# Sparse attention and a mixture of experts on one core: value tiles of the last batch by DMA, and another order of the same work

## The chip, the cores and the metric

The kernel runs on one core of a Trainium2 chip. The metric is device time in microseconds (us), as the median of several runs. TensorE (PE, with its weight loads as PEld), VectorE (DVE), ScalarE (ACT), GpSimd (POOL) and SyncE (SP, which here only issues loads and stores) each work through a queue of their own in order, and wait for one another by semaphores.

## The reference

Attention over 4 batches, 8 heads, 768 positions, head size 64. A query sees the keys less than 16 positions away and one summary key for each block of 32 (24 of them); then an expert layer works on the 128 best positions of each batch.

```
k_sum = k.reshape(B, H, nb, 32, D).max(axis=3)
v_sum = v.reshape(B, H, nb, 32, D).mean(axis=3)
scores = concat([where(|i - j| < 16, scale * q @ k.T, -1e9), scale * q @ k_sum.T + log(32)])
a = softmax(scores)
x = a @ concat([v, v_sum])            # heads side by side: x is 4 x 768 x 512
top = 128 largest of x[b] @ w_gate    # per batch
out[b] = x[b]
out[b, top] += sigmoid(x[b, top] @ w_gate) * (relu(x[b, top] @ w1) @ w2)
```

## The kernel before, in words

Two heads make a pair; there are 16 pairs, four to a batch, numbered n = 0 to 15. A pair is worked in three steps of 256 queries, so there are 48 steps, i = 0 to 47. Steps 0 to 35 go pair by pair (batches 0 to 2). In the last batch the steps go round: 36 to 39 are the first step of pairs 12 to 15, 40 to 43 the second, 44 to 47 the third.

The work of every engine is written as small named operations, and one string, `ORDER`, lists their names in the order in which they are issued. A letter behind a colon picks the engine where there is a choice (v VectorE, s ScalarE, g GpSimd). Each engine takes its own operations out of this one list, in this order, and an operation that waits holds up all that stand behind it on its engine. Nothing else plans the work.

The names, with the lines of the profile:

- `q`, `k`, `vt`: loads of a pair's queries, keys and turned values (L194, L190, L201), on SP's queue. Four buffers each for q and k, two for vt.
- `kmax` (L213, VectorE), `spr` (L216 or L175): block maxima of the keys, copied ahead of every slice of the key tile. `vsum` (L224 on VectorE, or five halvings on GpSimd, L230), `ms` (L254, L256): block sums of the values, and their means, written ahead of every slice of the value tile.
- `vx` (L265, TensorE): turns four value windows (positions to partitions) for one step of a pair, into the PSUM bank "m"; `vk` (L268) copies that to the value tile v. There are four value tiles.
- `S` (L289, TensorE): the scores of two steps, 32 products. `M` (L301, VectorE): adds the mask and takes the row minimum of the negated scores. `E` (L312 on ScalarE, four instructions; L315 on VectorE or GpSimd, one instruction): the exponent, or on VectorE and GpSimd the subtraction alone, with the exponent taken by the next copy. `sm` has two buffers, p three.
- `T` (L321, TensorE): turns p, four transposes; `V` (L326, L328): copies it out, to pt. `A` (L338, TensorE): p times the values, 16 products. `R` (L343), `N` (L354, L357): reciprocal and scaling into x.
- `ga`, `gq`, `gl` (L393, L383, L388, VectorE): gate sums of x. `rt`, `rk`, `rw`, `rr`: the row of a batch's sums, turned by TensorE (L400), written to memory and read back to all partitions (L406, L409). `cmp` (L427, L429, VectorE): comparisons, `rank` (L438), `oh`, `pick`, `pk`: the chosen positions. `gat` (L474, GpSimd): gathers their rows from memory.
- The expert layer: `fgp` (L537, GpSimd), `fx`, `f1` (L561), `ft`, `f2` (L614), `fo`, and `sca` (L628, GpSimd), which scatters the result. `w`, `wh`, `wl` load the weights and split them into a high and a low part (L495 or L175, L499).
- `zero`, `warm` (L663): products of zeros at the start, which write the bank "m". `clrv`, `onep`, `ones`: tiles set to constants.

Another way for the values is in the code and unused before: `VMODE[n] == "d"`. There a pair loads plain turned values (`vt`, for `vsum` alone, L199) and two halves of the finished value tile from memory (`v`, L206); the means are turned by one small transpose (`mt`, L237), scaled (`mk`, L240) and copied by DMA from SBUF into the two halves (`md`, L248). `vx`, `vk` and `ms` are not used for such a pair. A tile of 24 rows, two buffers, lies between `mk` and `md`.

Of the kernel before, what the change touches and what calls it, by code (L numbers as in the profile page):

```python
# [55 lines left out]
vx0.0 clrv0:g vk0.0:s E0:g M1.0:v onep0:g vx0.2 vk0.2:s T0 k1 kmax1:v spr1:g V0:s q1 S2 M2.0:v E1:g M3.0:v M3.1:v E3:g  # L56
M2.1:v vt1 vsum1:v vx0.1 vk0.1:s T1 k2 kmax2:v A0 R0:v V1:s A1 R1:v S4 M5.1:v E2:g ms1:s vx1.0 M4.0:v M4.1:v E4:g q2
N0:s vt2 T2 V2:s T3 spr2:s vk1.0:v vx1.1 vk1.1:s M5.0:v E5:v V3:s S6 k3 kmax3:v M6.1:v vx1.2 T4 M7.1:v N1:s M7.0:v
M6.0:v V4:s A2 R2:v vsum2:g A3 R3:v vk1.2:s q4 T5 q3 ms2:s vx2.0 V5:s vk2.0:s spr3:g S8 E7:v M9.0:v E6:g M8.0:v M8.1:v
N2:v T6 vx2.1 N3:s A5 R5:v clrv3:g vk2.1:s M9.1:v w1 E8:v vx2.2 N5:v V6:s T7 A4 vt3 wh3:g E9:g vsum3:v ms3:g R4:v V7:s  # L60
N4:v wl3:g k4 kmax4:v S10 M10.1:v vk2.2:s T8 V8:s vx3.2 M11.0:v M10.0:v A7 vk3.2:s A6 M11.1:v T9 V9:s vx3.0 spr4:g S12
R7:v N7:v k5 vk3.0:s A9 kmax5:v R6:v E11:v M13.1:v E10:g M12.1:v N6:s R9:v vx3.1 vt4 vsum4:g ms4:g vk3.1:s N9:v
casts:v T10 M12.0:v V10:s A8 vx4.2 vk4.2:s T11 k6 q5 V11:s spr5:g M13.0:v E13:s kmax6:v gate R8:v N8:v S14 spr6:s
E12:g A10 ga0.0:v ga0.1:v w0 M14.1:v q6 M15.1:v vt5 vx4.1 vk4.1:s T12 V12:s wh1:g wl1:g A11 vx4.0 vk4.0:s T13 V13:s
M15.0:v E15:s q7 M14.0:v S16 R10:v N10:v A12 E14:g R11:v N11:v k7 ga0.2:v ga0.3:v ga0.4:v A13 ga0.5:v rt0 rk0:s
M17.1:v M17.0:v T14 M16.1:v vsum5:g ms5:g vx5.0 V14:s vt6 T15 R12:v vk5.0:s M16.0:v vx5.1 vk5.1:s S18 kmax7:v E16:v
N12:v A14 R13:v spr7:s st0.0 N13:v E17:g V15:s T16 vsum6:g w2 wh5:g M19.1:v M18.1:v ms6:g V16:s vx5.2 wh2:s M18.0:v
M19.0:v E19:v vk5.2:s rw0 A15 R14:v E18:v wh4:s wl4:g S20 M20.0:v vx6.2 wl2:g vk6.2:s M20.1:v M21.0:v M21.1:v R15:v
T17 N15:v V17:s k8 vx6.0 vk6.0:s st0.1 N14:s kmax8:v rr0 cmp0.5:v vt7 T18 V18:s E20:g S22 M22.0:v A16 R16:v q8 k9
E21:s N16:s vx6.1 vk6.1:s vt8 M22.1:v T19 vsum7:v spr8:g M23.1:v ms7:s V19:s A17 R17:v cmp0.1:v A18 q10 R18:v N18:v  # L70
wh0:g wl0:g M23.0:v vx7.1 N17:s vk7.1:s cmp0.3:v kmax9:v T20 V20:s E22:g cmp0.4:v cmp0.2:v A19 R19:v N19:v vx7.0 E23:s
T21 cmp0.0:v vsum8:g rb0:v S24 M25.1:v M24.1:v V21:s T22 vk7.0:s vx7.2 V22:s M25.0:v vk7.2:s A20 R20:v M24.0:v T23
V23:s q9 rank0 rs0:v oh0:v A21 spr9:s S26 R21:v N21:v st0.2 pick0 pk0:v w3 wl5:g vt9 N20:v E24:s T24 M26.1:v E25:g
M27.1:v ms8:g V24:s M27.0:v vx8.0 vk8.0:s M26.0:v A22 R22:v N22:v k10 A23 T25 V25:s vx8.1 vk8.1:s gat0:g fgp0:g
ga1.0:v S28 vx8.2 vsum9:v vk8.2:s R23:v N23:v wh7:s A25 ga1.1:v fx0 fxh0:s kmax10:v E26:g T26 V26:s A24 R25:v wh6:g
M28.0:v ms9:s wl6:g f10.0 M28.1:v E28:s f10.3 spr10:s fxl0:v E27:g M29.1:v M29.0:v ga1.2:v w4 wh8:s ga1.3:v st1.0
vx9.0 vk9.0:s T27 V27:s ga1.4:v ga1.5:v w5 wh10:g E29:s wl7:v S30 rt1 rk1:s M30.0:v M31.0:v T28 V28:s f10.4 M31.1:v
E31:v wl10:g k11 vx9.1 N25:s vt10 k12 vsum10:v R24:v f10.1 f10.2 q11 wh11:g vk9.1:s rw1 N24:v kmax11:v spr11:s T29
vx9.2 M30.1:v E30:v vk9.2:s A26 st1.1 V29:s wl11:g A27 kmax12:v spr12:s fge0:s R27:v N27:v R26:v N26:v S32 M32.1:v T30
V30:s M32.0:v wh9:g ms10:g M33.1:v vx10.0 vk10.0:s w7 wh14:s A28 E32:v rr1 f10.5 vx10.1 R28:v fr0.0:s ft0.0 wl9:g  # L80
wl8:g w6 wh12:s wh15:g wl15:g M33.0:v cmp1.4:v T31 A29 N28:v A30 cmp1.1:v k13 S34 vt11 V31:s T32 R29:v N29:s vk10.1:s
A31 cmp1.0:v fr0.1:s ft0.1 V32:s cmp1.5:v cmp1.3:v st1.2 cmp1.2:v rb1:v R30:v wl14:g rank1 wh13:g wl13:g wl12:g
fh0.0:s fl0.0:v fh0.1:s rs1:v E33:g T33 vx10.2 vk10.2:s V33:s f20.0 oh1:v pick1 k15 M35.1:v fl0.1:v pk1:v gat1:g k14
vsum11:v f20.1 M35.0:v kmax13:v E35:g f20.2 ms11:s spr13:g vx11.0 vk11.0:s N30:v f20.3 R31:v N31:s kmax15:v vx11.2
vk11.2:s f20.4 fg0:v fx1 kmax14:v spr14:s M34.1:v spr15:s M34.0:v A32 fxh1:v fxl1:v q12 fgp1:g E34:g fge1:s A33 R33:v
N33:s ga2.0:v q13 S36 M37.1:v M37.0:v ga2.1:v R32:v M36.0:v T34 V34:s f20.5 f11.0 M36.1:v vx11.1 T35 fo0.0:v E37:s q14
vk11.1:s N32:v f11.1 q15 S38 E36:s A34 fg1:v M38.1:v M39.1:v R34:v V35:s A35 N34:v vt12 vsum12:g ms12:s ga2.2:v R35:v
N35:v sca0:g T36 V36:s vx12.0 vk12.0:s vt13 f11.3 vx12.1 M39.0:v f11.2 vk12.1:s fr1.0:s vx12.2 vk12.2:s f11.4 T37
ga2.3:v ga2.4:v ga2.5:v vsum13:v rt2 M38.0:v rk2:s V37:s S40 ms13:g vx13.0 vk13.0:s ft1.0 fh1.0:s E39:v E38:g M40.1:v
M40.0:v T38 vx13.2 vk13.2:s M41.1:v fl1.0:v f11.5 M41.0:v E41:v fr1.1:v V38:s vt14 vsum14:g ms14:g vx13.1 E40:v rw2  # L90
S42 M42.0:v rr2 vk13.1:s A36 R36:v N36:v A37 R37:v M43.0:v T39 V39:s vt15 M43.1:v cmp2.4:v vx14.0 vk14.0:s ft1.1
fh1.1:s T40 E43:g vx14.1 vk14.1:s M42.1:v E42:g vsum15:v ms15:g V40:s A38 R38:v st2.0 S44 N37:s T41 V41:s cmp2.3:v
vx15.0 vk15.0:s N38:v f21.0 M45.0:v M44.1:v cmp2.0:v M44.0:v M45.1:v T42 E45:g vx15.1 cmp2.1:v A39 R39:v cmp2.2:v
N39:s vk15.1:v A40 cmp2.5:v S46 A41 V42:s T43 rank2 f21.1 R41:v E44:g M46.0:v rb2:v rs2:v N41:s R40:v N40:v st2.2
V43:s T44 V44:s vx15.2 M47.1:v vk15.2:s oh2:v M46.1:v A42 A43 M47.0:v R42:v N42:s pick2 pk2:v R43:v N43:v T45 vx14.2
vk14.2:v fl1.1:v E46:g A44 R44:v st2.1 V45:s A45 E47:s T46 f21.2 f21.3 V46:s R45:v N45:s T47 V47:s gat2:g fgp2:g
gq3.0:v gl3.0:v gq3.1:v gl3.1:v ro3.0 ri3.0:s gq3.2:v gq3.3:v f21.4 gl3.2:v N44:s gl3.3:v cmp3.0:v f21.5 fo1.0:v
cmp3.1:v sca1:g fge2:s fx2 fxh2:s A47 R47:v N47:s fxl2:v A46 R46:v f12.0 f12.1 N46:v ro3.1 ri3.1:s f12.3 gq3.4:v
gq3.5:v gl3.4:v gl3.5:v ro3.2 ri3.2:s cmp3.2:v cmp3.3:v cmp3.5:v cmp3.4:v f12.2 fr2.0:s st3.1 f12.4 ft2.0 f12.5 rank3
fh2.0:s fl2.0:v fr2.1:s ft2.1 rb3:v rs3:v oh3:v pick3 pk3:v fh2.1:s fl2.1:v f22.0 st3.2 f22.1 f22.2 fg2:v f22.3 f22.4  # L100
st3.0 gat3:g fx3 fxh3:v f22.5 fo2.0:v f13.0 sca2:g f13.3 fxl3:v f13.1 f13.2 fr3.0:s f13.4 f13.5 fr3.1:s ft3.0 fh3.0:v
ft3.1 fl3.0:v fh3.1:v f23.3 f23.0 f23.1 fgp3:g fge3:s fl3.1:v f23.2 f23.4 fg3:v f23.6 f23.7 f23.5 f23.8 fo3.0:v f23.9
f23.10 f23.11 fo3.1:v sca3:g
"""


# [1 line left out]
def attn_moe(ctx: ExitStack, tc: tile.TileContext, q, k, v, vt, vs, w1, w2, cst, line, out, cap):  # L108
# [109 lines left out]
    def value_sums(e, n):  # L218
        vv = vtb[n % 2][:, 0:S].rearrange("p (u c) -> p u c", u=NU) if VMODE[n] == "d" else own(by_slot(vtb[n % 2]))
        vv = vv.rearrange("p u (m t) -> p u m t", t=BLK)  # L220
        vs_[n] = vss[:, n % 2]
        sums = vs_[n].rearrange("p (u m) -> p u m", u=NU)
        if e == "v":
            nc.vector.tensor_reduce(out=sums, in_=vv, axis=AX.X, op=ALU.add)  # L224
# [434 lines left out]
    def warm(e):  # L659

        ps = bank("m")
        for i in range(WARM):
            nc.tensor.matmul(out=ps, lhsT=zero.broadcast_to([128, 128]), rhs=zero.broadcast_to([128, 512]),  # L663
# [185 lines left out]
```

## Time and profile before

| | |
|---|---|
| time, median of 3 | 200.78 us (198.73 to 202.14) |
| the profiled execution | 202.29 us, of which the span of its instructions is 200.5 us |
| PE, PEld busy | 172.6 us (86%), 138.6 us (69%) |
| DVE, ACT, POOL busy | 157.0 us (78%), 100.3 us (50%), 99.1 us (49%) |
| DMA | 39.13 MB, 195 GB/s over the span |

In the profile, a row of a group names line, engine, operation, result and operands, the count behind x, and then busy us, mean ns of one, and the idle time just before with the engine that ended it. A row of the timeline starts with the start and the length in us. Busy time of an instruction that waits inside itself is counted as busy.

### The profile page before, as it was taken

To read this page: it belongs to the slowest core of one execution; us is meant where nothing else is said; L and a number is where in the kernel's file an instruction comes from. 1 tells how busy PE (TensorE), PEld (TensorE's weight loads), DVE (VectorE), ACT (ScalarE), POOL (GpSimd) and SP (SyncE) were. 2 spreads that over 40 slices of the span, in tenths; PEclk is the share of its full clock that TensorE was granted. 3 is DMA by queue.
4 is the path that set the end of the run, shared out by engine and by line. 5 is a ranking of instruction groups with operands and counts; after the bars stand their busy time and mean duration, and the time that the engine had idled before them with its cause. 6 is when DMAs were issued, how large, how long until landed. Compare 5 with 4: busy or idle time off the path is not lost.

```text
span 200.5 us, 6136 instructions
## 1 busy us (share of the span) xinstructions
PE 172.6 (86%) x2313; PEld 138.6 (69%) x2313; DVE 157.0 (78%) x705; ACT 100.3 (50%) x262; POOL 99.1 (49%) x134
## 2 busy tenths in 40 slices
...
GB/s 225 392 251 207 316 307 318 315 239 305 190 279 254 285 314 310 360 114 4 241 259 304 323 311 0 164 39 160 229 202 3 67 94 180 85 52 56 0 0 52
DMA packets 12753, 39.13 MB, mean 195 GB/s; under 512 B 1314, under 2 KB 1332, under 8 KB 12724
## 3 DMA queue, kind: packets, MB, share of 16 engines
...
q14 instruction: 11, 0.09, 0.1%
...
## 4 chain that ended last, share of the span: by engine, by line
DVE 47%; PE 30%; issue 8%; POOL 6%; DMA 3%; ACT 3%; POOLq 1%; SPq 0%; DVEq 0%; ACTq 0%
DVE sm L301 12%; DVE junkv L393 6%; DVE kss L213 5%; DVE lt L429 4%; DVE lt L427 4%; PE fa L614 4%; PE a L338 4%; DVE x L357 4%; PE m L265 4%; PE t L321 4%; DVE p L315 3%; PE fb L614 3%; PE sa L289 3%; DVE vss L224 3%; DMA vt<-in_vs_dram 3%
## 5 line engine op out<-in xcount | busy, mean ns | idle before, releaser
L315 POOL TENSOR_TENSOR p<-sm,mxs 128x480 f32<-128x480 f32 x25 | 25.7, 1030 | 26.8 <-DVE mxs L301 10.8
L268 ACT COPY v<-m 120x512 f32<-120x512 f32 x45 | 26.6, 591 | 21.6 <-PE m L265 21.5
L265 PE MATMUL m<-cs,vt 128*120 128x128 f32 x192 | 33.1, 300 | 2.9 <-ACT vt L254 1.3
L321 PE MATMUL t<-cs,p 128*120 128x128 f32 x192 | 32.1, 292 | 2.9 <-POOL p L315 1.7
L338 PE MATMUL a<-v,pt 121*64 121x65 f32 x768 | 30.5, 227 | 3.2 <-DVE x L357 1.3
L338 PEld LDWEIGHTS a<-v,pt 121*64 121x64 f32 x768 | 25.7, 139 | 9.5 <-issue 3.7
L328 ACT ACTIVATE pt<-t 120x512 f32<-120x512 f32 x38 | 22.9, 601 | 14.2 <-PE t L321 12.8
L289 PE MATMUL sa<-kb,qb 64*64 64x120 f32 x384 | 26.4, 276 | 2.8 <-DVE mxs L301 2.0
L265 PEld LDWEIGHTS m<-cs,vt 128*120 128x120 f32 x192 | 23.0, 148 | 8.4 <-ACT v L268 3.0
L301 DVE CUSTOM_DVE_ANT_0 sm<-sa,cs 128x120 f32<-128x120 f32 x96 | 22.1, 273 | 7.9 <-PE sb L289 4.3
L321 PEld LDWEIGHTS t<-cs,p 128*120 128x120 f32 x192 | 22.6, 145 | 6.8 <-POOL p L315 2.2
L289 PE MATMUL sb<-kb,qb 64*64 64x120 f32 x384 | 26.0, 276 | 0.2 <-DVE mxs L301 0.2
L301 DVE CUSTOM_DVE_ANT_0 sm<-sb,cs 128x120 f32<-128x120 f32 x96 | 22.2, 275 | 4.8 <-POOL p L315 2.3
L289 PEld LDWEIGHTS sa<-kb,qb 64*64 64x64 f32 x384 | 20.6, 137 | 7.3 <-DVE mxs L301 2.6
L289 PEld LDWEIGHTS sb<-kb,qb 64*64 64x64 f32 x384 | 20.4, 137 | 0.5 <-DVE mxs L301 0.5
L354 ACT ACTIVATE x<-a,rdens 128x64 f32<-128x64 f32 x72 | 16.8, 322 | 7.4 <-DVE rdens L343 7.4
L213 DVE TENSOR_REDUCE kss<-kb 128x24 f32<-128x768 f32 x16 | 15.1, 941 | 4.3 <-DMA kb<-in_k_dram 4.3
L393 DVE SCALAR_TENSOR_TENSOR junkv<-x,cs 128x512 bf16<-128x512 f32 x18 | 16.8, 934 | 1.0 <-ACT x L354 0.6
L301 DVE DVE_READ_ACCUMULATOR2_ANT mxs<- 128x1 f32 x192 | 15.5, 81 | 0.0
L628 POOL DMA_INDIRECT out_dram<-h,idx x4 | 4.2, 1051 | 20.5 <-DVE h L622 20.5
L312 ACT ACTIVATE p<-sm,mxs 128x120 f32<-128x120 f32 x40 | 12.5, 394 | 1.5 <-DVE mxs L301 1.5
L357 DVE TENSOR_TENSOR x<-a,rdens 128x256 f32<-128x256 f32 x30 | 12.6, 422 | 0.8
(126 smaller groups left out, 320.2 us busy)
## 6 DMA issues: line engine op xcount, KB each, us to landing
kb<-in_k_dram SPq DMA_DIRECT2D x16, 552.0 KB, 7.2
vt<-in_vs_dram SPq DMA_DIRECT2D x16, 552.0 KB, 4.5
...
```

Of the source, the lines that this page charges most:

```text
L213: nc.vector.tensor_reduce(out=ks.rearrange("p (u m) -> p u m", u=NU), in_=kv, axis=AX.X, op=ALU.max)
L265: nc.tensor.transpose(out=ps[0:NC, j * 128:(j + 1) * 128], in_=vt_[:, c0:c0 + NC], identity=ident)
L268: copiers[e](out=vwt[n % NVB][0:NC, 2 * g:2 * g + 2, :, :, 0:D], in_=vps[n, g][0:NC].rearrange("p (u a h d) -> p u a h d", u=2, a=2, h=2))
L289: nc.tensor.matmul(out=sc[k][h][par * QT:(par + 1) * QT, uu * NC:(uu + 1) * NC], lhsT=qt[rows, t * QT:(t + 1) * QT], rhs=kt[rows, window(t ...
L301: nc.vector.tensor_tensor_reduce(out=sm[:, j, :], in0=sc[i][h][:, uu * NC:(uu + 1) * NC], in1=cs[:, c0:c0 + NC], scale=-1.0 / D ** 0.5, sc ...
L315: engines[e].tensor_tensor(out=pb[i % 3], in0=sm, in1=mx.unsqueeze(2).broadcast_to([128, 4, NC]), op=ALU.subtract)
L321: nc.tensor.transpose(out=ps[0:NC, j * 128:(j + 1) * 128], in_=pb[i % 3][:, j, :], identity=ident)
L328: nc.scalar.activation(out=dst, in_=src, func=AF.Exp, scale=-1.0)
L338: nc.tensor.matmul(out=av[par * QT:(par + 1) * QT, j, :], lhsT=pt[0:NC + 1, j, par * QT:(par + 1) * QT], rhs=vw[n % NVB][0:NC + 1, par, u, ...
L354: nc.scalar.activation(out=x_(b, g)[:, j // 2, c:c + D], in_=av[:, j, 0:D], func=AF.Copy, scale=rden[:, j:j + 1])
L357: nc.vector.tensor_tensor(out=x_(b, g)[:, :, pr * 128:(pr + 1) * 128].rearrange("p u (h d) -> p u h d", h=2), in0=av[:, :, 0:D].rearrange( ...
L393: nc.vector.scalar_tensor_tensor(out=junkv, in0=x_(b, u // 2)[:, u % 2, :], scalar=1.0, in1=gate, op0=ALU.mult, op1=ALU.mult, accum_out=s_ ...
```

## The change

Three things. The pairs of the last batch, 12 to 15, get their value tiles by DMA (`VMODE` d). The warm products are 16 instead of 12. And `ORDER` is another list: the same operations but for those of the four pairs, in another order, with other engines where there is a choice. Among the changes of engine: `E` goes from 13 on VectorE, 10 on ScalarE and 25 on GpSimd to 5, 23 and 20; `vsum` from 9 on VectorE and 7 on GpSimd to 11 and 5; `wh` from none on VectorE to 3; two of three `onep` go to VectorE.

```
-WARM = 12
+WARM = 16
-VMODE = "pppppppppppppppp"
+VMODE = "ppppppppppppdddd"
 ORDER = """
-q0 clrv2:g zero:v warm k0 kmax0:v spr0:s vt0 onep1:g vsum0:v onep2:g clrv1:g ms0:s S0 cst M0.0:v M0.1:v ones:g M1.1:v
+clrv3:g onep0:v clrv1:g onep1:g clrv0:g onep2:v zero:v vt0 vsum0:g ms0:g k0 kmax0:v warm q0 spr0:s S0 cst vx0.0
+vk0.0:s k1 vx0.2 vk0.2:s casts:v M0.1:v M0.0:v E0:g T0 M1.1:v ones:g kmax1:v spr1:s M1.0:v q1 S2 V0:s E1:s M2.0:v
...
```

Line numbers behind `ORDER` are smaller by one in the changed kernel. Three places show what moved.

GpSimd, around the first gather (xe from out_dram, behind the pick of batch 0). Before; vt is written by `ms`, p by `E`, fprod by `fgp`, w1h and w1l by the weight split:

```order
L256 TENSOR_SCALAR vt_79<-vss 128x7x24
L474 DMA xe_126<-out_dram,idx_111 128x512
L537 TENSOR_TENSOR fprod<-xe_126,cs 128x512
L315 TENSOR_TENSOR p_98<-sm_94,mxs 128x480
L175 TENSOR_SCALAR w1h<-h 128x512
L499 TENSOR_TENSOR w1l<-h,w1h 128x512
```

Now:

```order
L255 TENSOR_SCALAR vt_79<-vss 128x7x24
L473 DMA xe_126<-out_dram,idx_111 128x512
L536 TENSOR_TENSOR fprod<-xe_126,cs 128x512
L255 TENSOR_SCALAR vt_80<-vss 128x7x24
L314 TENSOR_TENSOR p_96<-sm_95,mxs 128x480
L498 TENSOR_TENSOR w1l<-h,w1h 128x512
```

Behind the product fprod, which needs the gathered rows, stood the exponent of step 26; now the means of pair 9 (ms9) stand there, and the exponent of step 27 behind them.

TensorE, around the first row turn (rt0, which writes m from sss). Before; a is written by `A`, t by `T`, m also by `vx`:

```order
L338 MATMUL a_795<-v_75,pt_81 64x65 x8
L338 MATMUL a_811<-v_75,pt_82 64x65 x8
L400 MATMUL m<-cs,sss 6x128
L321 MATMUL t<-cs,p_98 120x128 x4
L265 MATMUL m<-cs,vt_80 120x128 x4
L321 MATMUL t<-cs,p_96 120x128 x4
```

Now:

```order
L320 MATMUL t<-cs,p_97 120x128 x4
L264 MATMUL m<-cs,vt_80 120x128 x4
L337 MATMUL a_918<-v_75,pt_83 64x65 x8
L399 MATMUL m<-cs,sss 6x128
L320 MATMUL t<-cs,p_98 120x128 x4
```

The row turn stood behind A11 and A12; it now stands behind T16, vx5.2 and A14, ahead of T17.

SP's queue in the last batch. Before, the loads of the last four pairs' values and what follows; line and rows are `rw2` and `rr2`, out_dram the stores of x:

```order
L201 DMA vt_79<-in_vs_dram 128x1104
L201 DMA vt_80<-in_vs_dram 128x1104
L201 DMA vt_79<-in_vs_dram 128x1104
L406 DMA line<-srow_109 6x128
L409 DMA rows<-line 128x768
L201 DMA vt_80<-in_vs_dram 128x1104
L363 DMA out_dram<-x_92 128x2x512
```

Now, from md12.1 on (v_75 to v_78 are the value tiles of pairs 12 to 15, from in_v_dram the loaded halves, from vs the means):

```order
L247 DMA v_75<-vs_88 24x6x130
L405 DMA line<-srow_109 6x128
L198 DMA vt_80<-in_vt_dram 128x768
L205 DMA v_78<-in_v_dram 96x780
L408 DMA rows<-line 128x768
L247 DMA v_76<-vs_89 24x6x130
L247 DMA v_77<-vs_88 24x6x130
L247 DMA v_76<-vs_89 24x6x130
L205 DMA v_76<-in_v_dram 96x780
L205 DMA v_77<-in_v_dram 96x780
L247 DMA v_77<-vs_88 24x6x130
L362 DMA out_dram<-x_92 128x2x512
```

Each pair has one load of its plain values, two of halves and two copies of means, where it had one load. Step 37 (A37) needs all four transfers into v_76.

More of the change, by code (lines that the diff above doesn't have):

```diff
@@ L54 @@
 ORDER = """
-q0 clrv2:g zero:v warm k0 kmax0:v spr0:s vt0 onep1:g vsum0:v onep2:g clrv1:g ms0:s S0 cst M0.0:v M0.1:v ones:g M1.1:v
[L56 to L103, printed above, removed]
+clrv3:g onep0:v clrv1:g onep1:g clrv0:g onep2:v zero:v vt0 vsum0:g ms0:g k0 kmax0:v warm q0 spr0:s S0 cst vx0.0
@@ new lines @@
+vk0.0:s k1 vx0.2 vk0.2:s casts:v M0.1:v M0.0:v E0:g T0 M1.1:v ones:g kmax1:v spr1:s M1.0:v q1 S2 V0:s E1:s M2.0:v
+M3.1:v vx0.1 vk0.1:s T1 V1:s vt1 M2.1:v E2:s M3.0:v E3:g vsum1:v ms1:s A0 R0:v S4 M4.1:v M5.0:v q2 T2 M5.1:v N0:s
+vx1.0 vk1.0:s vx1.1 V2:s k2 kmax2:v A2 M4.0:v E4:v vt2 vsum2:v A1 vk1.1:s vx1.2 vk1.2:s R1:v N1:v k3 kmax3:v T3 V3:s
+spr2:g S6 M6.1:v M6.0:v T4 E5:s M7.1:v M7.0:v R2:v ms2:g vx2.0 w0 A3 R3:v V4:s T5 wh1:v clrv2:g vk2.0:s vx2.1 vk2.1:s
+N3:s N2:v wh0:v q3 V5:v spr3:g S8 E6:g M8.1:v M8.0:v E7:g M9.1:v M9.0:v vx2.2 vk2.2:s T6 A4 R4:v N4:v vt3 A5 R5:v V6:s
@@ new lines @@
+k5 kmax5:v T7 S10 N5:v E9:s vsum3:g ms3:s E8:g M10.0:v V7:s vx3.1 vk3.1:s M10.1:v E10:g q4 spr5:s T8 V8:s A7 A6 vx3.2
+vk3.2:s k4 kmax4:v M11.1:v M11.0:v spr4:g T9 E11:g vt4 q5 vsum4:v R7:v N7:v R6:v N6:v S12 M12.0:v V9:s T10 V10:s vx3.0
+k6 vk3.0:s M13.1:v A8 M13.0:v E13:s T11 V11:s ms4:g R8:v wl0:g vx4.0 wl1:g M12.1:v E12:g S14 N8:v A10 kmax6:v M14.0:v
+vk4.0:s M14.1:v E14:g M15.1:v vx4.2 w1 wh3:s wl3:g T12 k7 M15.0:v kmax7:v A9 vk4.2:s R9:v V12:s R10:v N9:v S16 N10:s
+M16.0:v vx4.1 vk4.1:s spr6:s T13 V13:s vt5 vsum5:v ms5:s gate ga0.0:v E15:g A11 R11:v N11:s A12 M17.1:v T14 V14:s
@@ new lines @@
+vx5.0 vk5.0:s ga0.1:v M16.1:v E16:s spr7:g A13 q6 T15 V15:s q7 vx5.1 vk5.1:s M17.0:v S18 ga0.2:v ga0.3:v ga0.4:v R12:v
+N12:v st0.1 T16 E17:s ga0.5:v vx5.2 vk5.2:s M18.1:v V16:s M18.0:v E18:g A14 rt0 rk0:s T17 M19.1:v M19.0:v E19:g S20
+V17:s vt6 vsum6:v ms6:s vx6.0 st0.0 R14:v R13:v N13:v T18 A15 w2 wh4:g wh5:g wl4:g k9 vk6.0:s M20.0:v M21.0:v M20.1:v
+E20:s vx6.1 N14:v M21.1:v S22 R15:v rw0 N15:v wl5:g kmax9:v M22.0:v M22.1:v V18:s vk6.1:s wh2:g E21:s A16 R16:v T19
+V19:s wl2:g vt7 vsum7:v N16:s M23.1:v A17 vx6.2 vk6.2:s T20 R17:v A18 ms7:g vx7.2 V20:s T21 k8 vk7.2:s V21:s M23.0:v
@@ new lines @@
+E23:g N17:v rr0 A19 kmax8:v q8 spr8:g vx7.1 S24 R18:v N18:s E22:s cmp0.1:v vk7.1:s A20 cmp0.5:v q9 cmp0.3:v cmp0.2:v
+T22 V22:s vx7.0 vk7.0:s cmp0.4:v M24.1:v spr9:s cmp0.0:v M24.0:v M25.0:v E24:s rank0 M25.1:v E25:s R19:v T23 V23:s
+rb0:v vt8 vsum8:g ms8:g N19:v rs0:v oh0:v k10 R20:v N20:s S26 M27.0:v A21 pick0 pk0:v T24 vx8.1 st0.2 V24:s vt9 A22
+vk8.1:s R21:v N21:v A23 M26.0:v M26.1:v E26:s vx8.0 vk8.0:s gat0:g fgp0:g M27.1:v vsum9:v ms9:g R23:v S28 N23:s w3
+wh6:s w5 vx9.0 vk9.0:s E27:g T25 V25:s R22:v N22:v A24 wh10:s ga1.0:v vx8.2 vk8.2:s T26 V26:s A25 ga1.1:v ga1.2:v
```

27 lines of the change are left out of this document (added).

## The prediction

> **What bounds the kernel now.** I read the table of stretches first, then the chain of waits, then single rows of VectorE and GpSimd. Columns of the table: length, busy time of PE, PEld, DVE, ACT, POOL (instructions in brackets), granted clock, DMA share, GB/s.
>
> ```profile
> 12.00:75.00 63.00, 55.37 (x984) 45.45 (x983) 56.69 (x288) 39.81 (x104) 43.20 (x60) 0.94 0.81 271
> 75.00:125.00 50.00, 41.94 (x532) 34.15 (x531) 42.88 (x169) 26.52 (x69) 28.14 (x29) 0.90 0.64 225
> 125.00:175.00 50.00, 47.99 (x636) 39.04 (x634) 45.53 (x216) 29.01 (x80) 15.49 (x21) 1.00 0.36 123
> 175.00:200.50 25.50, 19.05 (x114) 15.84 (x114) 7.44 (x16) 2.48 (x6) 4.09 (x4) 0.99 0.09 31
> DVE 47%; PE 30%; issue 8%; POOL 6%; DMA 3%; ACT 3%; POOLq 1%; SPq 0%; DVEq 0%; ACTq 0%
> 74.68 0.63 PE L321 MATMUL t<-cs,p 128*120 128x128 f32 x4
> ```
>
> Behind a start of 12 us there are four stages. In A (12 to 75, steps 0 to 23; the last row is T24) VectorE is busy 90% and TensorE 88%. In B (75 to 125, the rest of batches 0 to 2 and the first expert block) it is 86% and 84%, and both wait together. In C (125 to 175, the last batch) TensorE has 96%, VectorE 91%. The tail is the last expert block, which the change leaves alone. VectorE carries 47% of the chain, so what shortens VectorE in A and B counts, and in C both must shorten.
>
> VectorE's time is partly waiting that is booked as work:
>
> ```profile
> 40.46 0.68 DVE L393 SCALAR_TENSOR_TENSOR junkv<-x,cs 128x512 bf16<-128x512 f32 x1
> 40.53 1.75 POOL L499 TENSOR_TENSOR w1l<-h,w1h 128x512 fp32r<-128x512 f32 x1
> 41.25 1.58 DVE L393 SCALAR_TENSOR_TENSOR junkv<-x,cs 128x512 bf16<-128x512 f32 x1
> 148.56 0.34 DVE L429 SCALAR_TENSOR_TENSOR lt<-rows,sss,tri 128x128 bf16<-128x128 f32 x1
> 149.90 1.98 POOL L315 TENSOR_TENSOR p<-sm,mxs 128x480 f32<-128x480 f32 x2 [2.65 <-DVE mxs L301]
> 149.92 1.12 DVE L429 SCALAR_TENSOR_TENSOR lt<-rows,sss,tri 128x128 bf16<-128x128 f32 x1
> 95.50 0.66 DVE L315 TENSOR_TENSOR p<-sm,mxs 128x480 f32<-128x480 f32 x1
> ```
>
> The same instruction takes 0.68 or 1.58, 0.34 or 1.12 us, and the long one is issued while GpSimd is inside an instruction that also reads two tiles. The first one is over about 0.6 us behind GpSimd's (42.83 against 42.28), its own length, so it has waited for nearly the whole of the other and then run.
>
> How much is that? Per stage, busy VectorE time of the three kinds (L429, L393, L315; in the first two each instruction has a short read behind it, so x12 is six):
>
> ```profile
> 12.00:75.00 63.00, 3.23 (x12) 0.94 0.81 271
> 75.00:125.00 50.00, 4.12 (x12) 0.90 0.64 225
> 125.00:175.00 50.00, 6.07 (x24) 1.00 0.36 123
> 12.00:75.00 63.00, 6.05 (x12) 0.94 0.81 271
> 75.00:125.00 50.00, 7.39 (x14) 0.90 0.64 225
> 12.00:75.00 63.00, 5.92 (x7) 13.26 (x13) 0.94 0.81 271
> 75.00:125.00 50.00, 3.05 (x3) 4.99 (x5) 0.90 0.64 225
> ```
>
> At the undisturbed 0.36 (0.34 and the end of its read), 0.68 and 0.66 us the excess is, in A, 1.1 + 2.0 + 1.3 = 4.4 us, in B 2.0 + 2.6 + 1.1 = 5.7, in C 6.07 - 12 x 0.36 = 1.8. Together 11.9 us of collisions.
>
> **The change part by part.** Rows for its prices:
>
> ```profile
> L312 ACT ACTIVATE p<-sm,mxs 128x120 f32<-128x120 f32 x40 | 12.5, 394 | 1.5 <-DVE mxs L301 1.5
> L268 DVE COPY v<-m 120x512 f32<-120x512 f32 x3 | 2.1, 686 | 0.2 <-PE m L265 0.2
> L224 DVE TENSOR_REDUCE vss<-vt 128x24 f32<-128x768 f32 x9 | 8.5, 945 | 1.7 <-DMA vt<-in_vs_dram 1.7
> L673 DVE TENSOR_SCALAR tri<-cs 128x128 bf16<-128x128 f32 x1 | 0.3, 276 | 0.0
> L674 DVE CAST tok<-cs 128x12 bf16<-128x12 f32 x1 | 0.3, 308 | 0.0
> L663 PE MATMUL m<-zero 128*128 128x512 bf16 x12 | 5.1, 614 | 0.9 <-DVE zero L657 0.9
> 125.00:175.00 50.00, 8.01 (x52) 5.73 (x52) 1.00 0.36 123
> 10.00:15.00 5.00, 4.27 (x44) 3.33 (x43) 1.34 (x8) 1.77 (x3) 2.50 (x4) 0.50 0.64 254
> ```
>
> *Start.* Four more warm products at 5.1 / 12 = 0.43 us are 1.7 us, and they start later, since two fills of pt now stand ahead of the zero tile on VectorE (VectorE has no such row; between 0.3, the 128-wide L673, and 0.7 us each, the 512-wide L268). But the first scores wait for k0 and q0, and q0 is now third in the load queue instead of first, so most of the 1.7 us lies in a wait. On the path are the two casts that now stand ahead of the first masked row: 0.28 + 0.31 = **+0.6 us**. If loads arrive early the products cost up to 1.7 instead.
>
> *Stage A.* VectorE's exponents go from 7 to 1 among steps 0 to 23 (-6 x 0.66 = -4.0), one value copy goes (-0.7), two value sums come (+1.9), a copy of pt (V5, +0.7) and two weight copies (wh0, wh1). No row has a weight copy on VectorE: between 0.28 (L673, a quarter of the width) and 0.69 us; I take 0.5, so +1.0. With the collisions gone: 56.7 - 4.4 - 4.0 - 0.7 + 1.9 + 0.7 + 1.0 = 51.2. ScalarE takes six exponents of four instructions, 12.5 / 10 = 1.25 us each: 39.8 + 7.5 less a copy or two, 46.5. TensorE keeps 55.4 and becomes the longest. At 92 to 94% of the stage, a little above the 90% that VectorE reached, the stage takes 59 instead of 63: **-4**. The ends are 0 (TensorE stays at 88%) and -7.6 (no gap at all). [...]
>
> One wait in A goes by the order alone. The row turn rt0 stood on TensorE behind A12 and waited for six gate sums on VectorE, with T14 and all else queued behind it; it now stands behind T16 and A14.
>
> ```profile
> PE m L400 <- DVE junkv L393: 4.0, 2, 2.9
> 75.43 1.15 POOL xe L474
> 76.58 5.80 issue
> 82.42 1.10 POOL fprod L537
> xe<-out_dram,idx POOLq DMA_INDIRECT x4, 4.4
> 75.79 1.15 PE L338 MATMUL a<-v,pt 121*64 121x65 f32 x32
> 73.04 0.31 PE L289 MATMUL sa<-kb,qb 64*64 64x120 f32 x1 [0.84 <-DVE mxs L301]
> 73.83 0.26 PE L289 MATMUL sb<-kb,qb 64*64 64x120 f32 x1
> ```
>
> Those 2.9 us are inside the 4 us, not beside them.
>
> *Stage B.* VectorE: three exponents fewer (-2.0), one weight copy more (+0.5), collisions -5.7: 42.9 to 35.7. ScalarE gets five exponents, 26.5 + 6.3 = 32.8. But the biggest hole stays. At 75.43 GpSimd starts the first gather and then stands before fgp0 until the rows land, 5.8 us behind the issue; E26 was queued there, and TensorE and VectorE ran dry. E26 is now on ScalarE, yet what is queued behind fgp0 is ms9, the means of pair 9, and TensorE's list has vx9.0, which needs them, only T24, two value turns, A22, A23 and S28 behind the pick. T24 took 0.63 us, a value turn is four transposes like it, A22 and A23 were the 1.15 of the row, and one set of 32 score products runs from 73.04 to 74.09: 3 x 0.63 + 1.15 + 1.05 = 4.1 us of cover from T24's start. The gather starts 0.75 us behind T24 (75.43 - 74.68) and lands 4.4 us (median) to 7.0 us later, and the product is another 1.1: 6.3 to 8.9 us, with the means still to come. So TensorE waits some 2 to 5 us again: the hole moves from E26 to ms9 and keeps its size. I credit B with less than half of VectorE's 7.2 us, **-3**; the ends are +2 (the hole grows) and -7.
>
> *Stage C.* 12 value turns of four transposes go: 48 of the 52 instructions in the row above, 8.01 x 48 / 52 = 7.4 us of TensorE. Four mean turns come, one transpose of 0.3 us each: 48.0 - 7.4 + 1.1 = 41.7. VectorE loses two value copies (-1.4) and 1.8 of collisions and gets one exponent (+0.65): 45.5 to 42.9, and is now the longest. At its 91% that is 47 us: **-3**; ends 0 and -7. ScalarE loses seven copies there and gets four small ones and two exponents, about even.
>
> *The loads that replace the turns.* Per pair one load of 384 KB instead of 552, two of 300 KB, and two small copies of the means. DMA is busy 36% in C, so bytes are no matter; order is. No row has such a copy; the nearest are these:
>
> ```profile
> vt<-in_vs_dram SPq DMA_DIRECT2D x16, 552.0 KB, 4.5
> 137.09 0.34 SPq L409 DMA_DIRECT2D rows<-line  x1
> 135.41 0.28 SPq L406 DMA_DIRECT2D line<-srow  x1
> ```
>
> A tiny write is through within 137.09 - 135.41 = 1.7 us, a load of 552 KB in 4.5; I take 3, between them, as the halves are of 300 KB. SP's queue holds v13.1 and v14.0 behind md14.0, which waits for mk14, which may only write its tile when md12.1 has landed, about when A36 runs. From there SP needs three issues of 0.4 us and the landing, 2.9 to 5.7 us, until A37 may start; TensorE has S42, T39, two f1 groups of four 512-wide products, S44, T40 and small turns in between, 2 x 1.05 + 2 x 0.63 + 8 products at up to the warm ones' 0.43, together up to 6.8 us. The cover holds, and I cost it at nothing; without it a late pair costs its wait in full, 1 to 3 us each for A37 to A39.
>
> Sum: +0.6 - 4 - 3 - 3 = -9.4 us. Against the profiled execution's 202.3 (span 200.5 and 1.8 around it) that is 192.9; that execution lay 1.5 above the median of 200.8, so on the median's scale **191.4, said as 191.5**.
>
> **The rivals.**
> 1. *ScalarE becomes the bound, slower.* Eleven exponents at 1.25 us instead of 0.65 sit in one in-order queue with the copies that feed TensorE. It decides where ScalarE can't run at 46.5 / 63 = 74% in A and 32.8 / 50 = 66% in B (now 63 and 53%). At 70 and 60% A takes 66.4 and B 54.7; with the start and -2 in C that is +6.7, **207.5**. Against it: in 60 to 70 us ScalarE already ran at over 90%:
> ```profile
> 60.00:65.00 5.00, 4.42 (x92) 3.59 (x90) 5.00 (x26) 4.70 (x18) 4.34 (x6) 1.00 0.75 261
> ```
> 2. *New waits take the place.* vx9.0 behind the gather and A37 to A39 behind the loads cost 2 to 3 us each over what I allowed: A -4, B 0, C 0, start +0.6: **197.4**.
> 3. *It does not keep them apart.* An order fixes neighbours in a queue, not times; if half a dozen steps slip, other pairs collide. Only the moves are left, -1, -1 and -2: **197.4** too. For it: GpSimd still has 20 of its 25 exponents, and 11 of the 16 value sums now stand on VectorE's queue, which moves all behind them. Against it: a fifth of the exponents, two sums and three weight copies have left GpSimd, so there is less to meet.
> 4. *The clock stays up.* The granted clock lies 6% of 63 and 10% of 50 us low, 8.8 us of cycles in A and B, and it fell after TensorE's holes (0.50 in the row of 10 to 15). If the holes are filled, 5 us more go: **186.5**. [...]
>
> **How the numbers follow.** Forecast 0.57, with a range of its own of 187.5 to 196; ScalarE 0.10; new waits 0.14; collisions kept 0.10; clock 0.09. A measurement of this kernel can tell about 2% (4 us) from no change: below 196.8 lie the forecast nearly whole, the clock and a little of the two at 197.4, 0.68; within 2% 0.22; slower 0.10. The range runs from 185 (the clock case, a little below) to 202 (both cases at 197.4 with their spread) and leaves out the slower case and the edges.
>
> **What would show it.** Right: L393, L429 and L315 on VectorE have means near 0.7, 0.36 and 0.66 us; C is about 3 us shorter, with VectorE busier than TensorE; rt0 waits under 1 us; vx9.0 waits for POOL's means. Wrong: waits of PE for ACT p (ScalarE), for DMA at A37 to A39 (the loads), L429 or L393 still above 0.5 and 0.9, or a start over 1 us later. I'm wrong, too, if TensorE has no more than 88% in A: then the collisions were hidden under other waits.

## The result, and the profile after

The changed kernel takes **190.6 us** (median of four runs, 189.9 to 191.6), beside 200.8 us for the kernel before on the same chip: a ratio of 0.953 with a 95% interval of 0.944 to 0.962. The profiled execution took 190.32 us, its span 188.5. All ratios compare undisturbed runs alone; in one series (the values by turns in the new list, the kernel without the low parts' reads, the twelve warm products, the first run of both letters) those of the kernel before lay at 197.6 to 199.3 us and its median at 201.8, so that a ratio there is nearer to one than the medians are.

In the kernel after, line numbers are smaller by one. The stages are cut at the same steps in both, at T0, T24, T34 and T47, since the times at which they stand have moved. First the kernel before, then the one after, in the table of stretches with the columns of the prediction:

```profile
0.00:11.93 11.93, 8.15 (x52) 4.07 (x53) 4.51 (x20) 2.54 (x4) 8.14 (x22) 0.88 0.85 325
11.93:74.68 62.75, 55.12 (x981) 45.20 (x981) 56.37 (x287) 39.81 (x104) 43.27 (x60) 0.94 0.81 270
74.68:123.46 48.78, 40.72 (x531) 33.10 (x527) 41.79 (x160) 25.41 (x67) 26.76 (x27) 0.90 0.67 233
123.46:162.10 38.64, 37.09 (x541) 30.86 (x538) 35.03 (x177) 23.53 (x64) 14.63 (x21) 1.00 0.38 124
162.10:200.50 38.40, 31.49 (x222) 25.39 (x220) 19.35 (x63) 9.06 (x25) 6.33 (x6) 1.00 0.15 56
```

```profile
0.00:11.40 11.40, 7.36 (x57) 3.59 (x57) 4.95 (x23) 2.20 (x3) 9.53 (x24) 1.00 0.85 321
11.40:66.73 55.33, 52.01 (x982) 42.70 (x981) 51.85 (x288) 46.05 (x129) 30.37 (x40) 1.00 0.89 302
66.73:107.62 40.89, 33.77 (x478) 27.51 (x475) 30.79 (x146) 28.62 (x81) 22.22 (x27) 0.87 0.73 254
107.62:151.08 43.46, 41.23 (x575) 33.06 (x573) 39.80 (x194) 24.50 (x76) 15.33 (x20) 1.00 0.69 209
151.08:188.50 37.42, 28.93 (x193) 23.31 (x193) 17.14 (x58) 6.93 (x16) 5.10 (x5) 0.97 0.12 43
```

The start is 0.5 us shorter, A 7.4, B 7.9, C 4.8 *longer*, the tail 1.0 shorter: 12.0 us of span. B, C and the tail must be read together. Between T34 and T47 the new list has five groups of second-layer expert products (f2), two A steps and a turn of gathered rows that stood ahead of T34, and two f2 groups, an A step and a turn that stood behind T47; thirteen value turns are gone from there. From T24 on it is 125.8 us before and 121.8 after, 4.0 less.

VectorE's two-input lines in the kernel after, grouped by line and form (count, busy us, mean ns of one), answer to the rows of collisions:

```profile
L392 DVE SCALAR_TENSOR_TENSOR junkv<-x,cs 128x512 bf16<-128x512 f32 x18 | 12.7, 706 | 1.1
L428 DVE SCALAR_TENSOR_TENSOR lt<-rows,sss,tri 128x128 bf16<-128x128 f32 x24 | 8.6, 362 | 0.0
L314 DVE TENSOR_TENSOR p<-sm,mxs 128x480 f32<-128x480 f32 x5 | 3.7, 735 | 0.1
L498 DVE TENSOR_TENSOR w2l<-hl,w2h 128x512 fp32r<-128x512 f32 x1 | 1.4, 1445 | 0.0
```

For the same lines before:

```profile
L393 DVE SCALAR_TENSOR_TENSOR junkv<-x,cs 128x512 bf16<-128x512 f32 x18 | 16.8, 934 | 1.0 <-ACT x L354 0.6
L429 DVE SCALAR_TENSOR_TENSOR lt<-rows,sss,tri 128x128 bf16<-128x128 f32 x24 | 13.2, 552 | 0.0
L315 DVE TENSOR_TENSOR p<-sm,mxs 128x480 f32<-128x480 f32 x13 | 11.0, 849 | 0.5
```

The means of the first two are at the undisturbed 0.7 and 0.36; that of the exponents is 0.74 beside the undisturbed 0.66, by one collision of 1.09 us. The low weight part now on VectorE met one too (1.45 us, where L506 of the same size takes 0.68 to 0.69). So list and letters together do keep the operations apart.

One long wait is left, where the prediction put it. Rows of the table of TensorE's waits, and of the chain, of the kernel after:

```profile
PE m L264 <- POOL vt L255: 7.4, 3, 6.2
...
PE m L399 <- ACT v L267: 0.6, 2, 0.3
```

```profile
68.43 1.15 POOL xe L473
69.57 6.22 issue
...
77.01 0.34 POOL vt L255
...
77.40 1.11 PE m L264 x4
```

GpSimd issues the gather, stands 6.2 us before the product of its rows, and the means of pair 9 behind it (L255) hold the value turn on TensorE.

### The profile page after: what moved, and what is told of

The parts are those of the page before. It is cut to its first block, busy times and chain, and to the rows that moved or that the text cites. A ratio compares the mean times of both kernels' runs of the same rounds, so it can differ in the third digit from the quotient of the medians.

```text
span 188.5 us, 6118 instructions
## 1 busy us (share of the span) xinstructions
PE 163.3 (87%) x2273; PEld 130.2 (69%) x2273; DVE 144.5 (77%) x702; ACT 108.3 (57%) x304; POOL 82.6 (44%) x114
## 4 chain that ended last, share of the span: by engine, by line
PE 34%; DVE 24%; POOL 13%; issue 11%; DMA 9%; ACT 4%; SPq 2%; POOLq 1%; DVEq 0%; ACTq 0%
DVE sm L300 6%; PE a L337 6%; PE t L320 5%; PE fb L560 5%; PE m L264 5%; POOL p L314 3%; PE fb L613 3%; PE fa L560 3%; PE sa L288 3%; POOL vhalf L229 3%; DMA hl<-in_w_dram 3%; DMA v<-vs 2%; POOL v L643 2%; DMA vt<-in_vt_dram 2%; DVE x L356 2%
## 5 line engine op out<-in xcount | busy, mean ns | idle before, releaser
L337 PE MATMUL a<-v,pt 121*64 121x65 f32 x768 | 31.8, 230 | 0.8 <-DVE x L356 0.3
L264 PE MATMUL m<-cs,vt 128*120 128x128 f32 x144 | 23.9, 291 | 9.2 <-POOL vt L255 7.4
L267 ACT COPY v<-m 120x512 f32<-120x512 f32 x36 | 21.3, 593 | 17.6 <-PE m L264 17.4
L314 POOL TENSOR_TENSOR p<-sm,mxs 128x480 f32<-128x480 f32 x20 | 20.8, 1047 | 20.7 <-DVE mxs L300 15.3
L311 ACT ACTIVATE p<-sm,mxs 128x120 f32<-128x120 f32 x92 | 28.7, 391 | 1.9 <-DVE mxs L300 1.8
L264 PEld LDWEIGHTS m<-cs,vt 128*120 128x120 f32 x144 | 16.2, 143 | 12.7 <-POOL vt L255 8.1
L327 ACT ACTIVATE pt<-t 120x512 f32<-120x512 f32 x25 | 14.9, 596 | 7.8 <-PE t L320 7.2
L212 DVE TENSOR_REDUCE kss<-kb 128x24 f32<-128x768 f32 x16 | 15.1, 942 | 4.0 <-DMA kb<-in_k_dram 4.0
L325 ACT COPY pt<-t 120x512 f32<-120x512 f32 x22 | 13.0, 593 | 6.4 <-PE t L320 6.3
L342 DVE RECIPROCAL rdens<-a 128x4 f32<-128x4 f32 x48 | 7.9, 173 | 9.9 <-PE a L337 9.9
L473 POOL DMA_INDIRECT xe<-out_dram,idx x4 | 4.1, 1024 | 22.6 <-DVE idx L468 21.8
```

The source lines that it names most:

```text
L212: nc.vector.tensor_reduce(out=ks.rearrange("p (u m) -> p u m", u=NU), in_=kv, axis=AX.X, op=ALU.max)
L264: nc.tensor.transpose(out=ps[0:NC, j * 128:(j + 1) * 128], in_=vt_[:, c0:c0 + NC], identity=ident)
L267: copiers[e](out=vwt[n % NVB][0:NC, 2 * g:2 * g + 2, :, :, 0:D], in_=vps[n, g][0:NC].rearrange("p (u a h d) -> p u a h d", u=2, a=2, h=2))
L311: nc.scalar.activation(out=pb[i % 3][:, j, :], in_=sm[:, j, :], func=AF.Exp, scale=-1.0, bias=mx[:, j:j + 1])
L314: engines[e].tensor_tensor(out=pb[i % 3], in0=sm, in1=mx.unsqueeze(2).broadcast_to([128, 4, NC]), op=ALU.subtract)
L327: nc.scalar.activation(out=dst, in_=src, func=AF.Exp, scale=-1.0)
```

## The experiments

**Parts of the change without the others.** Its three large parts are the values by DMA, the letters and the order of the list; three kernels leave one or two of them out; two more follow below.

The values by DMA in the list before:

```diff
-VMODE = "pppppppppppppppp"
+VMODE = "ppppppppppppdddd"
-vt12 vsum12:g ms12:s
+vt12 v12.0 v12.1 vsum12:g mt12 mk12:s md12.0 md12.1
-vx12.0 vk12.0:s vt13
+vt13 v13.0 v13.1
```

(and so for pairs 13 to 15).

> The kernel before with one part alone: the values of pairs 12 to 15 by DMA, all else in the old order with the old engines. Theory (TensorE has 96% in the last batch, so work taken from it is time): TensorE's busy time falls by about 6 us (144 value turns instead of 192, four mean turns more) and the time by 3 to 6, to 195 to 198. Rival (VectorE, 91% busy, holds the last batch as well): TensorE's busy time falls by the same, the time by less than 1.5, 199.5 or more. Second rival (the copies of the means land late): TensorE waits for DMA ahead of A, over 201.

Measured: 216.5 us, 1.078 (1.065 to 1.091) times the kernel before. TensorE's waits:

```profile
PE m L236 <- DVE vss L223: 5.4, 1, 5.4
PE m L236 <- POOL vss L229: 4.8, 1, 4.8
```

and a piece of its chain:

```profile
138.11 0.33 PE m L236
...
138.47 0.28 ACT vs L241
...
138.76 0.82 SPq L247
...
140.53 3.19 DMA vt<-in_vt_dram
...
143.85 1.00 POOL vhalf L229
...
146.67 0.40 PE m L236
```

This is one ring: means' product on TensorE (L236), copy on ScalarE, the means' sends in SyncE's queue (L247), and only then the next load of sums, which stands behind them in that queue; then the sums, and the next pair's product, for which TensorE stops with everything behind it. The step that did this on ScalarE or GpSimd before (ms) held up nothing on TensorE behind T34. The two waits, 10.2 us, are the larger part of the 15.1 us by which the stage from T34 to T47 is longer (53.74 against 38.64); the rest isn't assigned.

The letters after on the list before, 99 steps changed, nothing moved (for example):

```diff
-E2:g ms1:s
+E2:s ms1:s
```

> The kernel before, its list kept word for word, with only the engine letters of the changed one (exponents 5 VectorE, 23 ScalarE, 20 GpSimd and so on; values of the last batch as before, 12 warm products). Theory (the relief of VectorE is half moves, half collisions): VectorE's busy time falls by 6 to 10 us, with L393 and L429 still above 0.8 and 0.45 us at times, and the time by 2 to 5: 196 to 199. Rival (the order keeps the engines apart and the letters alone do nothing, or ScalarE binds): 200 or more.

Measured: 225.3 us, 1.116 (1.104 to 1.128). The list after, its values by DMA and its warm products, with the letters before (again 99 steps):

```diff
-E2:s
+E2:g
```

> The changed kernel's list, values by DMA and 16 warm products, but the engine letters of the kernel before wherever both have the operation. Theory: with eight more exponents on VectorE and five more on GpSimd collisions are back (L392 above 0.8 us, L428 above 0.45), VectorE is busy 6 to 12 us longer than in the changed kernel, and the time is 195 to 200. Rival (the order alone carries the gain): under 193.

Measured: 223.3 us, 1.103 (1.091 to 1.116). Neither has one wait that explains it. VectorE's waits of the first, the longest ones:

```profile
DVE sm L301 <- PE sb L289: 14.4, 6, 6.1
DVE rdens L343 <- PE a L338: 11.4, 8, 2.7
DVE sm L301 <- POOL p L315: 7.0, 3, 3.3
...
DVE sm L301 <- ACT p L312: 4.8, 4, 2.6
```

VectorE waits for every engine, a few microseconds each: in in-order queues a step that takes longer on another engine, or stands behind others there, holds up its neighbours; that the delays add up round the ring of scores, exponents, turns and sums is my reading of these many waits, not shown by itself. The largest part stands in A, 71.9 us in both kernels, against 62.8 before and 55.3 after. What I expected of all three was wrong: the parts aren't terms of a sum.

**The values by DMA, placed better in the list before.**

```diff
-vt12 v12.0 v12.1 vsum12:g mt12 mk12:s md12.0 md12.1
+vt12 vsum12:g vt13
-vt13 v13.0 v13.1
+mt12 mk12:s v12.0 v12.1
+md12.0 md12.1
```

(and so for pairs 14 and 15).

> The kernel before with its list and letters and the values of pairs 12 to 15 by DMA, as in the run at 216 us, but placed otherwise: each pair's sums are loaded as soon as the pair before is summed, the product for the means and its copy stand where the first value products stood, the values follow it, and the means are sent at the place of the second value products. In the run at 216 us TensorE waited 10.2 us at the means' products, and SyncE's queue held each next load of sums behind the means' sends (vt, sums, product, copy, send, next vt, in one chain). Theory: that chain was the cost, not the DMA; with it cut the value products that go (12 x 0.65 us) show, up to 8 us behind T34: 192 to 197. Rival: the list before has no room for it at any such place, and TensorE waits for the landings of values or means instead: 200 to 210, with waits on v<-v or on the means' product above 3 us.

Measured: 209.1 us, 1.044 (1.036 to 1.051): the rival. The ring is cut (7 us better), but now the landing of the means is late. TensorE's waits, in a profiled execution of 214.7 us:

```profile
PE a L337 <- DMA v<-vs: 9.7, 3, 7.0
PE m L399 <- DVE junkv L392: 6.2, 3, 2.9
```

So at neither of the two places tried had the list before room for both, the means' product and the landing; the list after has, but for one wait of 1.4 us at a means' product.

**The change without the values by DMA.**

```diff
-VMODE = "ppppppppppppdddd"
+VMODE = "pppppppppppppppp"
-mt12
+ms12:s
...
+vx12.0 vk12.0:s
...
+vx12.1 vk12.1:s
```

(the loads `v` and the sends `md` go; and so for pairs 13 to 15, put in by hand).

> The changed kernel, with its list and letters, but the values of pairs 12 to 15 turned on the core again (twelve groups of four products of about 0.65 us on TensorE and twelve copies of 0.6 us on ScalarE come back, four groups for the means and the value loads by DMA go; the steps are put in by hand behind the work of T36 to T44). Theory of the prediction: behind T34 TensorE is the bound (41.2 of 43.5 us busy), so the kernel grows by the products that come back less the means, 12 x 0.65 - 4 x 0.28 = 6.7 us, or 5 to 6 of them: about 196. Rival, that the rest of the change made the 10 us and the values nothing: 190 to 192. Second rival, after the first group of runs, that any list whose steps were not placed for its work loses far more: above 200, with TensorE waiting in many places.

Measured: 198.3 us (196.6 to 200.8), 0.997 (0.989 to 1.005): no faster than the kernel before that one can tell, and 8 us over the changed kernel. Its stretches B and C:

```profile
66.39:104.12 37.73, 32.61 (x479) 26.62 (x475) 31.79 (x146) 28.37 (x81) 22.20 (x23) 0.95 0.81 280
104.12:157.60 53.48, 47.96 (x618) 39.10 (x616) 40.46 (x194) 30.30 (x85) 17.33 (x23) 0.97 0.37 124
```

TensorE has 6.7 us more in C than in the changed kernel (47.96 against 41.23), just the worked-out 12 x 0.65 - 4 x 0.28, and C is 10 us longer, part of which may be my placing. So the new list without the values is fast up to T34 and gives it back behind it: the expert work that it has there needs the room that the value turns leave. (B is even 3.2 us shorter than in the changed kernel, whose steps there are the same but for the size of two loads; its gather was over sooner, 4.5 us behind the issue instead of 6.3, and TensorE waited 4.1 us behind it instead of 6.2.)

**The collisions alone, in the kernel before.**

```diff
-        engines[e].tensor_tensor(out=l, in0=part, in1=h.bitcast(F32), op=ALU.subtract)
+        if e == "g":
+            for _ in range(3):
+                nc.gpsimd.memset(l.bitcast(F32), 0.0)
+            return
+        engines[e].tensor_tensor(out=l, in0=part, in1=h.bitcast(F32), op=ALU.subtract)
```

> The kernel before, with GpSimd's thirteen or so subtractions for the low weight parts replaced by three memsets each of the same tile (the low parts are left out of the result: zeros stand there), so that GpSimd stays busy at the same places without reading two inputs beside VectorE. Theory, collisions cost time: VectorE's excess beside these subtractions (6 to 7 us of the 11.9 us in all) goes, and where VectorE is late for TensorE the span falls by 3 to 5: 196 to 199, with the means of the two-input lines on VectorE lower. Rival, collisions hidden behind other waits: 200 to 202 although the means fall. Second rival: three memsets take much less time than a subtraction, GpSimd has room, and both fall together; then GpSimd's busy time, 99 us before, says so.

Measured: 196.3 us, 0.983 (0.972 to 0.994), some 3.4 us by the ratio. GpSimd stays as busy (102.3 us; three memsets of 0.525 us for one subtraction of about 1.3). Its stretch B:

```profile
71.16:118.73 47.57, 39.38 (x530) 31.98 (x527) 38.38 (x162) 25.80 (x68) 29.04 (x46) 0.93 0.67 235
```

VectorE has lost 3.4 us there (41.79 to 38.38), the stage 1.2 against this profile of the kernel before (48.78 to 47.57). But the two kernels with the values by DMA in the list before have the same steps in this stage and took 50.90 and 49.75 us, against which it is 3.3 and 2.2. Such differences are as large as the effect, so the stage doesn't settle what part of its length a collision is worth. Over the whole kernel VectorE is busy 6.4 us less (157.0 to 150.7) for the 3.4 us of time. The memsets differ in one thing more: GpSimd stood 3.1 us for ScalarE's high parts ahead of the subtractions, and memsets need no high part.

**Twelve warm products instead of sixteen**, in the changed kernel.

```diff
-WARM = 16
+WARM = 12
```

> The changed kernel with twelve warm-up products as before instead of sixteen. Theory of the prediction, that four products cost about what they take and keep nothing: within 0.5 us of the changed kernel, 190 to 191, the granted clock in the first 70 us at 1.00 all the same. Rival, that they hold the clock up until T0 and through the first stage: the clock dips between 5 and 15 us as it did before, and the time is 192 to 194.

Measured: 189.7 us, 0.950 (0.937 to 0.962) times the kernel before; the changed kernel has 0.953. T0 stands at 11.39 us (11.40 with sixteen), and the clock is 1.00 from 5 to 20 us in both. The four products change nothing.

**The wait for the gather.** Two letters in the changed kernel, first one, then both:

```diff
-M27.1:v vsum9:v ms9:g
+M27.1:v vsum9:v ms9:s
```

> The changed kernel with one letter changed: the means of pair 9 (ms9) on ScalarE instead of GpSimd, where they stand behind the product that waits for the gather. Theory (TensorE's 6.2 us wait at vx9.0 is for these means alone): the wait goes, the clock does not fall to half behind it, and the time falls by 3 to 6 us, to 185 to 188. Rival (the next thing behind the gather, the exponent of step 27 on GpSimd, holds the same engines): the wait moves to T27 and the time stays within 1.5 us of 190.6.

```diff
-w5 vx9.0 vk9.0:s E27:g
+w5 vx9.0 vk9.0:s E27:v
```

> The changed kernel with two letters changed: the means of pair 9 on ScalarE (as in the run at 184.3 us) and the exponential's product of block 27 on VectorE instead of GpSimd. In that run GpSimd waited 6.25 us for the gathered rows with block 27's product queued behind (TensorE waited 2.6 us for it, VectorE 2.5 us), and the granted clock fell to 0.82 for ten microseconds. Theory: both waits and the dip go, 2.5 to 3.5 us, giving 181 to 182. Rival: VectorE, 79% busy, takes over 0.7 us at a full place and a next wait ends there: 184 to 185.

> The changed kernel with only the means of pair 9 on ScalarE, beside the next run on one chip. Theory: the first of the two letters brings what there is, 184 to 185, and the second one's 2.6 us is taken back behind T34, where the span of that stage grew from 42.5 to 43.7 us. Rival: the second letter keeps 1 to 2.5 us, and this one is slower by that.

> The changed kernel with both letters (the means of pair 9 on ScalarE, the product of block 27 on VectorE). Theory: 184, the same as with one letter. Rival: 182 to 183.

Measured: one letter 184.3 us, 0.907 (0.897 to 0.917), and again 186.2, 0.926 (0.919 to 0.933); both letters 184.2, 0.928 (0.917 to 0.939), and again 184.4, 0.922 (0.916 to 0.928). Side by side the second letter brings 1.8 us between medians and 0.8 by the ratios, within the intervals, so in the time it can't be told from nothing. With one letter TensorE still waits 2.6 us at T27 for the exponent E27, which stands behind the gather on GpSimd; with both that wait is gone. The stages from T24 to T34 and from T34 to T47, with one letter and then with both:

```profile
66.47:103.33 36.86, 32.73 (x478) 26.40 (x474) 31.65 (x146) 28.41 (x82) 21.78 (x26) 0.95 0.85 290
103.33:145.83 42.50, 41.23 (x575) 33.19 (x573) 39.32 (x194) 24.42 (x76) 15.01 (x20) 1.00 0.70 213
```

```profile
66.62:99.97 33.35, 31.08 (x478) 25.17 (x475) 31.70 (x147) 28.59 (x82) 20.44 (x22) 1.00 0.93 314
99.97:143.68 43.71, 40.88 (x574) 32.82 (x573) 39.54 (x194) 24.46 (x76) 15.56 (x20) 1.00 0.68 208
```

B falls from 40.89 us to 36.86 to 33.35 and its clock rises from 0.87 to 0.95 to 1.00; C gives back 1.2 of the second step. In the profiles of the repeat B is 37.36 and 33.87 us at a clock of 0.95 and 0.97, and C gives back 0.2, so the second letter does shorten B by 3.5 us both times. The version with both letters beats both kernels: 0.922 of the kernel before.

## Why the prediction was right, point by point

The forecast was 191.5 us, the time is 190.6. The sum came out nearly right, but several of its terms did not, and that their errors offset each other is luck: start and A came out 4.5 us better than forecast, about 3.6 of it, by my estimate from T24 (74.68 us there, 71.04 in an execution without the fall), because the clock fell in the one execution that was taken as the base, and from T24 on it came out 2.0 worse.

- **The start**, +0.6 forecast, -0.5 between the two profiles. The profile of before is one of an execution in which the clock fell; the table of stretches there, from 5 to 15 us:

```profile
7.50:10.00 2.50, 1.23 (x22) 0.89 (x12) 2.19 (x14) 0.34 (x1) 0.29 (x1) 0.82 1.01 407
10.00:12.50 2.50, 1.77 (x9) 1.47 (x8) 1.30 (x7) 0.91 (x2) 2.25 (x4) 0.50 1.01 410
12.50:15.00 2.50, 2.50 (x37) 1.86 (x36) 0.04 (x1) 0.86 (x2) 0.26 (x1) 0.50 0.26 99
```

  The kernels with the values by DMA in the list before (at 216 us) and without the low parts have the same steps up to T24 (the latter but for the memsets) and don't show it: the clock of A is 0.97 in both instead of 0.94, their T0 stands at 10.30 and 10.36 us, their T24 at 71.04 and 71.16 instead of 74.68. The one at 209 us has these steps too and was late (T0 at 12.57, T24 at 75.54). Against the two executions without the fall the start is 1.0 to 1.1 us longer: the term's sign was right, and its size near. Its path was wrong: T0 stands on TensorE behind the second value turn (10.91 us), and the chain to that turn runs through GpSimd's three fills of value tiles, its block sums and means, and the first turn and its copy, not through the casts (the exponent behind them is ready at 10.86). So the size is luck.
- **Stage A**, -4 forecast, -7.4 measured. The step that was off is "TensorE keeps 55.4": it fell to 52.0, which is 55.1 x 0.94, the clock before against 1.00 after. What that execution had lost by its clock came on top. Against the undisturbed stage, this row of the kernel at 216 us,

```profile
10.30:71.04 60.74, 53.35 (x983) 43.99 (x981) 55.52 (x288) 39.60 (x104) 44.27 (x62) 0.97 0.87 294
```

  A is 5.4 us shorter. TensorE has 94% of it (92 to 94 forecast), VectorE 51.85 us (51.2 forecast), ScalarE 46.05 (46.5 forecast).
- **Stages B and C**, -6 together forecast with no change in the tail, -4.0 measured from T24 on; B alone -7.9 and C +4.8 where each had -3. The working took both as if every step kept its stage; the order had moved expert work and A steps across T34 and T47. The step that failed in B is "the hole moves from E26 to ms9 and keeps its size": before, TensorE stood 2.1 us for the gathered rows and 1.4 us for E26; after, it waited 6.2 us for ms9, where I gave 2 to 5. The gather itself took about as long (7.4 us from its start to the product, 7.0 before), but it began 1.7 us behind T24 instead of 0.75, and the value turn came another 1.6 us behind the product's start. DMA was full while the gather was under way, and the clock fell behind the hole, in the table of stretches after:

```profile
70.00:75.00 5.00, 1.17 (x34) 0.82 (x32) 4.65 (x15) 2.15 (x8) 0.00 (x0) 0.85 1.01 366
75.00:80.00 5.00, 2.60 (x21) 2.27 (x22) 0.04 (x2) 1.14 (x3) 2.40 (x3) 0.50 0.35 141
80.00:85.00 5.00, 4.76 (x41) 3.83 (x39) 2.57 (x20) 3.08 (x7) 1.41 (x2) 0.63 0.01 2
```

  With the one letter that takes the means of pair 9 from behind the gather, the profiled span is 5.2 us shorter, and 4.1 in the repeat. That is more than the 2 us by which B and C fell short. The place and the cause were right; the size of the wait was not. What the lower clock behind it costs is small here: with twelve warm products the wait was 6.4 us and the clock of B 0.92 instead of 0.87, and B took 40.75 us beside 40.89.
- **C's longest engine.** "VectorE is now the longest" was wrong: TensorE has 41.23 of 43.46 us, VectorE 39.80. And the values by DMA, credited with C's 3 us, are worth some 8 in the new list, by the run without them: the list puts other work in the room that they leave.
- **Collisions.** The 11.9 us are all but gone, as said. Whether the list does it or the letters is not separated: with the letters alone the means of L393, L429 and L315 on VectorE are 0.82, 0.40 and 0.65 us (0.93, 0.55 and 0.85 before), with the new list and the letters before 0.77, 0.40 and 0.86, so that each without the other takes away over half of the excess, in kernels that wait more and are over 10% slower. Nor were the collisions worth their length: the run without the low parts' reads has VectorE 6.4 us less busy for 3.4 us of time. The credit of less than half in B is neither shown nor refuted by that run's stage (1.2 to 3.3 us for 3.4).
- **The loads**, costed at nothing behind their cover. The landing stands on the chain after, and TensorE has work nearly throughout it:

```profile
129.85 4.39 DMA v<-vs
...
134.28 0.68 PE a L337 x14
```

  Two issues (L205, 0.5 and 1.1 us) and a landing of 4.4 us are 6.1, a little over the 2.9 to 5.7 forecast and under the cover of 6.8: TensorE's waits for values come to under half a microsecond. The run at 209 us, with the same loads in the list before, shows the price without cover: 9.7 us in three waits.
- **The gate's turn rt0** no longer waits for the gate's sums, 2.9 us before: TensorE's waits at L399 are two of 0.3 us, for ScalarE's copies, under 1 us as forecast.
- **Weight copies on VectorE** took 0.42 us where no two-input instruction of GpSimd was under way ahead of it, and 0.61 and 0.87 us beside GpSimd's two-input exponents (0.5 assumed). So the two beside them were 0.2 and 0.45 us longer, in sum 0.6.

The rivals: ScalarE ran at 83% of A and 70% of B, the shares at which I had set its deciding point or above, and TensorE waits for none of its exponents. New waits came at one place of two. Collisions did not stay. "The clock stays up" held in A and at the start (the granted clock is 1.00 to 70 us), yet not through the four products, as the run with twelve shows; that the fuller TensorE in the new list did it (94% of A at a clock of 1.00, 88% at 0.94 before) is my guess, not shown by itself. In B the clock stayed down (0.87, 0.90 before).

What stays open: why the same steps of the list before are late at T0 in two of their four profiles (before, where the clock fell to 0.50, and the one at 209 us) and not in the others; and how the gain of A divides between fewer exponents on VectorE and fewer collisions, since no run changes one without the other in the new list.
